# Limiting the expert weight loads in flight to three, in a kernel of chunk attention, a swish layer and a mixture of experts

## The chip, the cores and the metric

The program runs on one core of a Trainium2 chip. The metric is the device time of one execution in microseconds; the time before is the median of three executions.

## What is computed

Three stages, one behind the other, all in float32 (inputs q, k, v of 2 x 8 x 768 x 64):

```python
# 1. attention in chunks of 32 queries: 16 keys to the left, 8 to the right, 8 memory keys
a = softmax(q_c @ concat(mem_k, k_ctx).T / sqrt(D))
x = a @ concat(mem_v, v_ctx)                      # -> 1536 tokens x 512
# 2. a dense layer
h = x @ w_in                                      # 512 x 2048
x = (h * sigmoid(1.702 * h)) @ w_out              # 2048 x 512
# 3. a mixture of 8 experts, top 1, at most 384 tokens for each
e = argmax(x @ w_gate); gate = softmax(x @ w_gate)[e]
y = relu(x_e @ w1[e]) @ w2[e]                     # 512 x 1024, 1024 x 512
out[token] = gate * y
```

## The kernel before, in words

TensorE gets fp32 precision from pairs of a rounded high part and a low part (float32r tiles): each product is three matmuls, high by high, high by low, low by high. So each weight that comes from memory is first turned into such a pair: ScalarE writes the high part (`hi`, L295), VectorE subtracts it from the raw words for the low part (`lo`, L300).

The first two stages take the span up to about 330 us. They run by an order written out by hand (`ORDER`) and by a loop over units of the dense layer. The third stage runs from about 340 us: `expert_parts` makes the pieces of one expert, and the loop at the end of the kernel (L1407) goes through the eight experts. For each it issues the gathers of the next expert's token rows on GpSimd (`load`, L827, an indirect DMA), then the weight loads that have a buffer, and then the expert itself. How many tokens an expert has is known only on the chip, so `both` (L1090) builds the code in two arms under a branch, and at run time every engine branches by itself to one of them: `first_of_two` (L1045), `first_of_narrow` (L1059) or `first_of` (L1037) for the first layer, then `thirds_first` (L1111), `after_arms` (L1142) and `second` (L1148) for the rest. The first layer's results stand in four PSUM buffers (L1389), from which ScalarE and VectorE evict them.

The expert weights are 64 loads (`pieces`, L209) of 512 KB, eight for each expert: four of `w1`, four of `w2`. `w_load` (L228) issues them on SP's queue (L241) into raw buffers taken from `free_raw` (four from L327, four more from L1396). `w_a` (L303) converts the oldest piece in flight and gives its raw buffer back, which is what lets the next load be issued: a load waits at L241 for the VectorE subtraction that last read its buffer. `w_next` (L347) calls this from set places in the arms, so the order of the conversions on ScalarE and VectorE, and of the loads on SP, is fixed when the program is built. `not_before` (L242) is one more wait that already exists, for a gather. From about 340 us on, SP issues nothing but these loads.

`w_state` and `w_back` (L356, L359) let `both` build the second arm from the same state as the first; both arms issue the same loads.

Of the kernel before, what the change touches and what calls it, by code (L numbers as in the profile page):

```python
# [38 lines left out]
AHEAD = 4  # L39
EARLY = 12  # L40
KEEP = 4
KEEPS = (3, 7, 8)
HALF = P // 2
HEAD2 = 2
# [48 lines left out]
def kernel(  # L93
# [40 lines left out]
    def wait_for(i, j):  # L134

        tc.add_manual_dep(i, j.name, mybir.DependencyInfo(mybir.DependencyClass.Sync, mybir.DependencyReason.DATA),
                          reason="wait_for")
# [77 lines left out]
    pool32 = []  # L215
    free_raw = []
    not_before = []

    def w_dst(name, i, z):

        t = where[name][:, z]
        if name[0] == "wi":
            return t.rearrange("p (c f) -> p c f", f=512)[:, :, i * P:(i + 1) * P]
        if name[0] == "wo":
            return t.rearrange("p (c f) -> p c f", f=P)[:, 4 * i:4 * i + 4]
        return t.rearrange("p (c f) -> p c f", f=512)[:, 2 * i:2 * i + 2]

    def w_load():  # L228

        if w_at[0] >= w_end[0]:  # L230
            return False
        name, i, src = pieces[w_at[0]]
        if not w_can_load():
            return False
        if len(name) == 2:
            w_slot(name)
            raw = w_pools["raw"].tile([P, KC, P, 2], I32, tag="raw", name="raw")
            nc.sync.dma_start(out=raw.rearrange("p c f z -> p c (f z)"), in_=src)
        else:
            raw = free_raw.pop(0)  # L240
            dma = nc.sync.dma_start(out=raw, in_=src).ins  # L241
            for i0 in not_before:  # L242
                wait_for(dma, i0)
        w_at[0] += 1
        flight.append(Piece(name=name, i=i, raw=raw))
        return True
# [5 lines left out]
    def w_slot(name):  # L252
        if name not in where and free_slots:
            where[name] = free_slots.pop(0)
        return name in where
# [90 lines left out]

    def w_next(e, keep=KEEP):  # L347

        name, i = (flight[0].name, flight[0].i) if flight else pieces[min(w_at[0], w_end[0] - 1)][:2]
        if not flight or name[1] * 8 + 4 * (name[0] == "w2") + 2 * name[2] + i >= 8 * e + 8 + keep:  # L350
            return False
        w_step()
        w_loads(8 * F // 512)
        return True

    def w_state():  # L356
        return w_at[0], list(flight), list(free_slots), list(free_raw), dict(where), set(ready)

    def w_back(state):  # L359

        w_at[0] = state[0]
        flight[:], free_slots[:], free_raw[:] = state[1:4]
        for now, was in ((where, state[4]), (ready, state[5])):
            now.clear()
            now.update(was)

    def w_loads(n):
        while len(flight) < n and w_load():
            pass

    def w_can_load():
        if w_at[0] >= w_end[0]:
            return False
        name = pieces[w_at[0]][0]
        return bool(name in where or free_slots) if len(name) == 2 else bool(free_raw)
# [440 lines left out]
    def expert_parts(e, ep, tp, cnt):  # L816
# [212 lines left out]
        def steps(part):  # L1029
            while w_next(e, KEEPS[part]):  # L1030
                pass

        def pump_one(i):
            for _ in range(PUMPS1[i]):
                w_next(e, KEEPS[0])

# [8 lines left out]
        def first_of_two():  # L1045
# [3 lines left out]
            for fc in range(F2):  # L1049
# [3 lines left out]
                if fc in PUMPS:  # L1053
                    w_next(e, KEEPS[0])
            with tc.issue_after(after_mm):
# [3 lines left out]
        def first_of_narrow():  # L1059
# [4 lines left out]
            for fc in range(F2):  # L1064
# [17 lines left out]
                if fc in PUMPS:  # L1082
                    w_next(e, KEEPS[0])
            for z in range(2):
# [4 lines left out]

        def both(cond, yes, no):  # L1090

            before = w_state()
            with tc.If(cond) as some:  # L1093
                yes()
            after = w_state()
            w_back(before)
            with some.Else():
                no()
            assert w_state() == after

        def wide_h(b):
# [9 lines left out]
        def thirds_first():  # L1111

            y_of(1 if e == 0 else 0)
            assert NCB == 3
            for b in range(2, NCB):
                hT_of(b)
                xs_of(b)

                def first():
                    both(cnt[ex] > b * P + HALF, lambda: wide_h(b), lambda: small_h(b))  # L1120

                both(cnt[ex] > b * P, first, start2)
            for j in range(F // 512):
                w_free(("w1", e, j))

        def rest(b):

            if b == NCB:
                return
            y_of(b)  # L1130

            def some():
                gate(b)
                both(cnt[ex] > b * P + HALF, lambda: full(b), lambda: small2(b))

            both(cnt[ex] > b * P, some, lambda: skip(b))
# [55 lines left out]
    with ExitStack() as st:  # L1192
# [34 lines left out]
        def after_attention(_):  # L1227
# [24 lines left out]
            a=lambda p: loaded[p].abs(), b=lambda p: loaded[p].max(), f=lambda p: loaded[p].shift(),  # L1252
# [242 lines left out]
```

## Time and profile before

| what | us |
|---|---|
| median of three runs | 531.24 |
| lowest and highest run | 529.93, 532.84 |
| profiled execution, device time | 531.82 |
| its span, first to last instruction | 530.0 |
| TensorE busy (95% of the span) | 505.2 |
| VectorE, ScalarE, GpSimd busy | 317.6, 279.0, 113.6 |

The time of the profiled execution is 1.8 us longer than the span of its instructions. "PE" is TensorE's matmuls and "PEld" its weight loads, "DVE" is VectorE, "ACT" ScalarE, "POOL" GpSimd, "SP" the engine whose queue issues the loads; a "q" behind a name is that engine's sequencer. "issue" as the end of a wait means that the engine waited for nothing the profile shows. The clock column is the granted share of TensorE's full clock: 1.00 is 2.4 GHz, 0.50 is 1.2 GHz.

### The profile page before, as it was taken

To read this page: it belongs to the slowest core of one execution; us is meant where nothing else is said; L and a number is where in the kernel's file an instruction comes from. 1 tells how busy PE (TensorE), PEld (TensorE's weight loads), DVE (VectorE), ACT (ScalarE), POOL (GpSimd) and SP (SyncE) were. 2 spreads that over 40 slices of the span, in tenths; PEclk is the share of its full clock that TensorE was granted. 3 is DMA by queue.
4 is the path that set the end of the run, shared out by engine and by line. 5 is a ranking of instruction groups with operands and counts; after the bars stand their busy time and mean duration, and the time that the engine had idled before them with its cause. 6 is when DMAs were issued, how large, how long until landed. Compare 5 with 4: busy or idle time off the path is not lost. (4 is left out here: it accounts for less than half of the span.)

```text
span 530.0 us, 10749 instructions
## 1 busy us (share of the span) xinstructions
PE 505.2 (95%) x4085; PEld 434.9 (82%) x4089; DVE 317.6 (60%) x633; ACT 279.0 (53%) x573; POOL 113.6 (21%) x108
## 2 busy tenths in 40 slices
PE   8799999999999999999999999999899799969994
PEld 4689898899989998998888888778787688958883
DVE  5999894587982372222256435549345787854851
ACT  2798887856742342212254333557345676645740
POOL 3334442342310120000000000252002322311211
PEclk9899999999999999999999999999999899979998
DMA  8888564043450004000059311499553868973000
GB/s 319 311 305 307 180 217 144 2 160 109 130 160 1 1 1 160 1 0 1 21 163 306 110 40 28 136 329 381 184 182 108 288 239 258 334 251 122 5 28 29
DMA packets 38761, 80.19 MB, mean 151 GB/s; under 512 B 3865, under 2 KB 10009, under 8 KB 38682
## 3 DMA queue, kind: packets, MB, share of 16 engines
q1 hardware_dynamic: 36010, 70.66, 39.0%
q0 software_dynamic: 2672, 8.47, 4.9%
q8 instruction: 50, 0.82, 0.6%
q14 instruction: 29, 0.24, 0.1%
HBM read 69.63 MB, written 9.75 MB: 150 GB/s over the span
## 5 line engine op out<-in xcount | busy, mean ns | idle before, releaser
L547 PEld LDWEIGHTS psh<-xT,w 128*128 128x128 f32 x1152 | 147.0, 188 | 8.3 <-ACT g L566 0.7
L590 PE MATMUL acc<-w,g 128*128 128x512 f32 x576 | 153.0, 400 | 0.0
L547 PE MATMUL psh<-xT,w 128*128 128x256 f32 x1152 | 151.7, 281 | 0.2 <-ACT g L566 0.2
L590 PEld LDWEIGHTS acc<-w,g 128*128 128x128 f32 x576 | 100.7, 188 | 19.4 <-issue 2.1
L562 ACT ACTIVATE sg<-psh 128x256 f32<-128x256 f32 x96 | 36.7, 383 | 126.4 <-PE psh L547 124.4
L300 DVE TENSOR_TENSOR w<-raw,w 128x1024 fp32r<-128x1024 f32 x64 | 76.0, 1221 | 29.7 <-ACT w L295 25.8
L570 DVE TENSOR_TENSOR g<-sg,g 128x256 fp32r<-128x256 f32 x78 | 38.1, 490 | 80.3 <-ACT g L566 77.7
L295 ACT ACTIVATE w<-raw 128x1024 fp32r<-128x1024 f32 x64 | 65.2, 1054 | 5.1 <-PE psy L1002 3.5
L1002 PE MATMUL psy<-w,hT 128*128 128x512 f32 x240 | 60.9, 412 | 5.0 <-issue 5.0
L1002 PEld LDWEIGHTS psy<-w,hT 128*128 128x128 f32 x240 | 46.5, 197 | 16.6 <-issue 5.7
L601 DVE SCALAR_TENSOR_TENSOR x<-acc,x 128x512 f32<-128x512 f32 x36 | 24.1, 685 | 20.8 <-PE acc L590 20.8
L566 ACT ACTIVATE g<-psh 128x256 fp32r<-128x256 f32 x96 | 36.2, 379 | 0.0
L827 POOL DMA_INDIRECT xr<-rows,taker x18 | 24.4, 1358 | 33.9 <-ACTq L1093 18.8
L1072 PE MATMUL psh<-xs,w 128*128 128x256 f32 x96 | 27.8, 290 | 3.7 <-issue 3.7
L1070 PE MATMUL psh<-xs,w 128*128 128x384 f32 x96 | 30.0, 351 | 0.0
L725 POOL DMA_INDIRECT y<-rows,taker x1 | 1.2, 1228 | 123.8 <-DVE cnt_i L732 123.8
L300 POOL TENSOR_TENSOR w<-w,w 128x512 fp32r<-128x512 f32 x12 | 16.8, 1403 | 42.2 <-ACT w L295 42.2
L290 POOL TENSOR_TENSOR w<-w,rest 128x512 int32<-128x512 int32 x13 | 17.6, 1356 | 34.2 <-DVE w L276 28.1
L276 DVE SCALAR_TENSOR_TENSOR w<-raw,w 128x512 int32<-128x512 int32 x32 | 24.7, 778 | 0.3
L265 ACT ACTIVATE w<-raw 128x512 f32<-128x512 f32 x32 | 21.3, 676 | 6.6 <-DMA raw<-in_w_out_dram 5.8
L295 ACT ACTIVATE w<-w 128x512 fp32r<-128x512 f32 x32 | 19.7, 627 | 9.6 <-POOL w L290 5.0
L1012 POOL DMA_INDIRECT out_dram<-y,taker x10 | 12.2, 1224 | 56.0 <-ACT y L1011 32.9
(163 smaller groups left out, 661.2 us busy)
## 6 DMA issues: line engine op xcount, KB each, us to landing
raw<-in_w_dram SPq DMA_DIRECT2D x64, 512.0 KB, 7.0
raw<-in_w_out_dram SPq DMA_DIRECT2D x16, 512.0 KB, 4.6
raw<-in_w_in_dram SPq DMA_DIRECT2D x16, 512.0 KB, 3.7
vt<-in_v_dram SPq DMA_DIRECT2D x12, 512.0 KB, 4.5
kt<-in_k_dram SPq DMA_DIRECT2D x12, 368.0 KB, 5.5
qt<-in_q_dram SPq DMA_DIRECT2D x12, 256.0 KB, 4.6
out_dram<-blank SPq DMA_DIRECT2D x12, 256.0 KB, 2.7
rows<-x SPq DMA_DIRECT2D x5, 520.0 KB, 4.9
```

The source lines that it names most:

```text
L276: nc.vector.scalar_tensor_tensor(out=self.w, in0=self.words()[1], scalar=-0x40000000, in1=self.w, op0=ALU.bitwise_and, op1=ALU.bitwise_or)
L295: nc.scalar.activation(out=w_dst(self.name, self.i, 0), in_=w, func=AF.Copy)
L300: eng.tensor_tensor(out=lo, in0=w, in1=hi.bitcast(F32), op=ALU.subtract)
L547: nc.tensor.matmul(ps, lhsT=w[:, wz, c, i * P:(i + 1) * P], rhs=xT[tb][:, xz, c, :], start=n == 0, stop=n == 3 * KC - 1)
L562: nc.scalar.activation(out=sg_t[u], in_=h_t[u], func=AF.Silu, scale=1.702)
L566: g_last[:1] = [nc.scalar.activation(out=g[:, 0], in_=h_t.pop(u), func=AF.Silu, scale=1.702).ins]
L570: lo = eng.tensor_tensor(out=g[:, 1], in0=sg_t.pop(u), in1=g[:, 0].bitcast(F32), op=ALU.subtract)
L590: nc.tensor.matmul(acc_t[tb][s], lhsT=g[:, gz, s * P:(s + 1) * P], rhs=w[:, wz, wi, :], start=i == 0 and n == 0, stop=u == last_of(k, tb) ...
L827: return nc.gpsimd.indirect_dma_start(out=t, out_offset=None, in_=rows[:, :], in_offset=bass.IndirectOffsetOnAxis(ap=taker[:, b, ex:ex + 1 ...
L1002: nc.tensor.matmul(ps, lhsT=h[:, hz, fc, o:o + P], rhs=w[:, wz, fc % 4, :], start=fc == 0 and n == 0, stop=fc == F2 - 1 and n == 2)
L1070: nc.tensor.matmul(ps[:, :2 * n].rearrange("p (z n) -> p z n", z=2), lhsT=w[:, 0, c, f0:f0 + P], rhs=t[:, :, c, :n], start=c == 0, stop=False)
L1072: mm = nc.tensor.matmul(ps[:, :2 * P], lhsT=w[:, 1, c, f0:f0 + P], rhs=t[:, 0, c, :], start=False, stop=c == KC - 1)
```

## The change

A list `on_way` holds the last expert loads. Each new load waits, besides what it waited for before, until the load three ahead of it in the order has landed; at most three are then in flight. Where two arms of a branch issue a load each, the list keeps both, and what comes behind waits for the one that ran. The order of all instructions stays.

```diff
+ON_WAY = 3
...
     not_before = []
+    on_way = []
...
             raw = free_raw.pop(0)
             dma = nc.sync.dma_start(out=raw, in_=src).ins
-            for i0 in not_before:
+            on_way.append((dma,))
+            for i0 in not_before + [i for some in on_way[:-ON_WAY] for i in some]:
                 wait_for(dma, i0)
+            del on_way[:-ON_WAY]
...
         def both(cond, yes, no):
 
-            before = w_state()
+            before, ways = w_state(), list(on_way)
             with tc.If(cond) as some:
                 yes()
-            after = w_state()
+            after, ways_yes = w_state(), list(on_way)
             w_back(before)
+            on_way[:] = ways
             with some.Else():
                 no()
+            on_way[:] = [a if a == b else a + b for a, b in zip(ways_yes, on_way)]
             assert w_state() == after
```

## Rows read from the trace of the kernel before

**Rows 1.** The page: span and busy time

```profile
span 530.0 us, 10749 instructions
PE 505.2 (95%) x4085; PEld 434.9 (82%) x4089; DVE 317.6 (60%) x633; ACT 279.0 (53%) x573; POOL 113.6 (21%) x108
```

**Rows 2.** Waits of PE, 340 to 530: us in total, times, longest

```profile
PE psy L1002 <- issue: 5.0, 3, 4.4
PE psh L1072 <- issue: 3.7, 1, 3.7
PE psh L918 <- DVE xs L909: 1.5, 1, 1.5
```

**Rows 3.** Timeline of PE at both: start, us, what, [idle before]

```profile
417.63 0.58 PE L1072 MATMUL psh<-xs,w 128*128 128x256 f32 x1 [3.69 <-issue]
...
463.69 1.03 PE L846 MATMUL pst<-ident,xr 128*128 128x128 f32 x8
469.09 1.19 PE L1002 MATMUL psy<-w,hT 128*128 128x512 f32 x2 [4.37 <-issue]
```

**Rows 4.** Windows: PE, PEld, DVE, ACT, POOL busy, PEclk, DMA share, GB/s

```profile
415.30:416.30 1.00, 0.00 (x0) 0.00 (x0) 1.00 (x2) 1.00 (x2) 0.69 (x2) 1.00 0.75 212
416.30:417.60 1.30, 0.00 (x0) 0.00 (x0) 1.30 (x2) 0.79 (x1) 1.30 (x1) 0.86 0.78 145
417.60:420.70 3.10, 3.07 (x12) 3.07 (x13) 2.03 (x3) 0.79 (x2) 0.31 (x1) 0.51 1.00 360
420.70:424.00 3.30, 3.30 (x24) 3.30 (x24) 2.03 (x4) 1.70 (x5) 0.00 (x0) 1.00 1.04 394
...
464.50:466.30 1.80, 0.22 (x3) 0.00 (x0) 1.51 (x3) 1.80 (x4) 0.00 (x0) 1.00 1.05 387
469.10:475.30 6.20, 6.20 (x15) 4.85 (x16) 3.50 (x3) 2.95 (x3) 0.00 (x0) 0.50 0.64 212
475.30:483.10 7.80, 7.80 (x35) 6.14 (x33) 1.45 (x3) 1.82 (x4) 1.01 (x1) 1.00 0.62 197
```

**Rows 5.** DMA queues, 415.3 to 416.3, then 466.3 to 467.5: packets, MB, share

```profile
q8 instruction: 1, 0.02, 6.1%
...
q8 instruction: 1, 0.02, 5.8%
```

**Rows 6.** Loads issued 452 to 460 (seven), then at 406.1, 410.7, 455.3, 459.4

```profile
DMA to landing us min/median/max: 9.2/10.2/10.7
...
DMA to landing us min/median/max: 4.1/4.1/4.1
...
L241 SPq DMA_DIRECT2D raw<-in_w_dram x1: 368/368/368, 410.7 to 410.7; - x1
DMA to landing us min/median/max: 5.1/5.1/5.1
...
L241 SPq DMA_DIRECT2D raw<-in_w_dram x1: 368/368/368, 455.3 to 455.3; - x1
DMA to landing us min/median/max: 10.3/10.3/10.3
...
L241 SPq DMA_DIRECT2D raw<-in_w_dram x1: 367/367/367, 459.4 to 459.4; - x1
```

**Rows 7.** The load issued at 357.4

```profile
DMA to landing us min/median/max: 8.1/8.1/8.1
```

**Rows 8.** Timeline of ACT, 359 to 368

```profile
364.38 2.22 ACT L295 ACTIVATE w<-raw 128x1024 fp32r<-128x1024 f32 x2 [0.27 <-ACTq L1093]
366.81 1.06 ACT L295 ACTIVATE w<-raw 128x1024 fp32r<-128x1024 f32 x1
```

**Rows 9.** PE's lines by form from 363.5 to 374.9: busy us, mean ns

```profile
L879 PE MATMUL psh<-xs,w 128*128 128x256 f32 x96 | 11.7, 283 | 0.0
```

**Rows 10.** Timeline of SP, 196 to 276

```profile
199.73 1.93 SPq L241 DMA_DIRECT2D raw<-in_w_dram  x4
262.10 6.13 SPq L1279 DMA_DIRECT2D out_dram<-blank  x3
```

## The prediction, made before the change was run

> **What bounds the kernel now.** I read the page first: in a span of 530.0 us TensorE is busy for 505.2 [rows 1]. So a change off TensorE's path pays only where TensorE idles, or where its clock is low. The change acts on the expert loads, nearly all of which are issued from 340 us on, so the next view is TensorE's waits from 340 to 530 us. Two waits stand out, 4.37 and 3.69 us, both ended by "issue", which is nothing that the profile names; the next is 1.5 us, for VectorE [rows 2, 3]. No wait of TensorE names a weight conversion or a load's landing. Loads are early enough already; the change can't gain by bringing weights sooner. If it gains, it is in the two "issue" waits.
>
> What are they? In both the engine has just gone into another arm or out of one (at 413.5 it enters `first_of_narrow`, at 464.6 it leaves `first_of_two`), and within each exactly one packet moves on the instruction queue q8: 6.1% and 5.8% of sixteen engines over 1.0 and 1.2 us, that is 0.98 and 1.11 us [rows 5]. I read them as code being fetched. By the Trainium skill (Runtime: NRT & Kernel Launch, "Instruction fetch mechanics") a taken branch whose target is outside the two resident pages must first fetch a page by DMA; the trace agrees, with its one packet in each wait. After each the clock falls to 1.2 GHz: 12 matmuls take 3.07 us at a clock of 0.51, against 24 in 3.30 us at 1.00, a loss of 3.07 - 12 x 0.138 = 1.4 us; 15 take 6.20 us at 0.50, against 35 in 7.80, a loss of 6.20 - 15 x 0.223 = 2.9 us [rows 4]. All that there is to win is 3.7 + 4.4 + 1.4 + 2.9 = 12.4 us.
>
> **The change part by part.** *How many loads it holds.* Taking each load's issue and landing from the trace, 27 of the 64 are issued before the load three ahead has landed. Example: the load at 455.3 lands 10.3 us later, at 465.6; the one three behind it is issued at 459.4 and would now wait until 465.6, 6.2 us more [rows 6]. So the change does what it says, in three bursts (347 to 370, 415 to 423 and 452 to 459 us); elsewhere the wait is met before it is asked.
>
> *What a held load loses.* A load alone lands in 4.1 us, in the burst in 9.2 to 10.7 [rows 6]. The burst's extra is queueing: the DMA moves 387 GB/s there [rows 4], 0.524 MB in 1.35 us. Three in flight, each taking 4.1 us, give one in 1.37 us, practically the same rate. A load that is issued 6 us later would have stood 6 us in the queue, so its landing hardly moves. I cost this at nothing; the cover is the lone load's 4.1 us. If held loads went on taking 8 us, see the second rival.
>
> *What is queued behind the wait.* SP issues nothing but these loads from 340 us on. Early on, the fourth load (issued near 201) would wait some 2.5 us for the first, and behind it SP's next transfer is at 262 [rows 10]: nothing. Some 27 waits on SP's sequencer cost other engines nothing. GpSimd's gathers are on a queue of their own; TensorE waits for none now.
>
> *What the two stalls gain.* At 413.5, TensorE stops; the next held load is the one at 414.8, and the one three ahead of it (issued 410.7) lands 5.1 us later, at 415.8, so it is held 1 us only, and the DMA is not full in this stall (0.75 to 0.78 busy, 145 to 212 GB/s) [rows 4, 6]. Nothing in front of that fetch changes: 0. At 464.6 four loads are in flight and the DMA is full (1.05, 387 GB/s) [rows 4]; with the change three are, and the queue is nearly drained just then. What is a full queue worth to a fetch? The nearest rows are the two stalls themselves: 4.37 us with it full, 3.69 with it three quarters busy [rows 3]. I take the difference, 0.7 us. Upper bound: if the second stall's clock loss shrinks to that of the first, 2.9 - 1.4 = 1.5 us more, 2.2 in all; I do not take it, since a stall of 3.7 us lost clock as well and no row shows a stall of this kind that did not. Lower bound: 0.
>
> Against even the 0.7 speaks the Trainium skill (DMA: Bandwidth & Descriptors, "Queues, rings and completion order"): each DMA engine takes turns between the queues that have work, packet by packet, so the depth of the loads' queue would not hold the fetch back. The trace agrees in part: the packet had moved by 467.5, while the load issued at 459.4, landing after 9.2 us at the earliest, was still under way [rows 5, 6]. By that rule alone the sum would be 0.
>
> The sum: 531.8 (the profiled execution) - 0.7 = 531.1. That execution is 0.6 above the median of 531.24, so for a median I take 530.5.
>
> **The rivals.**
>
> *No effect.* Fetches take turns whatever the depth, and landings stay. For it: the stall at 413.5, nearly as long with the queue not full. Then the time stays at 531.2. It lies within 0.5% as the forecast does, and the two differ only in the second stall.
>
> *A large gain.* The fetch is served only when loads in front of it have moved, and its completion is late for the same reason. Then the second stall is cut to well under half or vanishes with its clock loss: 4.4 + 2.9 = 7.3 us, 524; were the first cut too, 12.4, 519. For it: both stalls lie in a burst. Against it: the first had at most three loads in flight when it began, so three are enough for 3.7 us. Half of the second gone (2.2 + 1.5 = 3.7 us) gives 527.5.
>
> *Slower: three in flight are too few.* In the burst from 347 to 370 us gathers share the DMA, and a load takes 8.1 us [rows 7]. If a held load went on taking that, three would give one in 2.7 us instead of 1.35. The load issued at 357.4 lands at 365.5 and is converted at 366.8 [rows 7, 8], with 1.3 us to spare; from the first held load of this burst to it there are five, so it would be 5 x 1.35 - 1.3 = 5.4 us late. ScalarE works in order, so the evictions behind this conversion (the L882 rows' line) would be late by as much. What covers TensorE are four PSUM buffers of 12 matmuls: 11.7 us for 96 [rows 9], 1.46 each, 5.9 in all if all were free; with half of them free some 2.5 us of stall come through, and the clock loss of one stall (1.4): 535. It decides from the point at which a held load takes over 3 x (1.35 + 1.3 / 5) = 4.8 us. Against it: much of the 8.1 us is queueing behind other loads, which the wait removes.
>
> **How the numbers follow.** Half a per cent (2.7 us) is about what a measurement of this kernel can tell from no change; the three runs before span 2.9 us. Forecast, 0 to 2.2 us gained at the second stall: 0.45. No effect: 0.24, within 0.5% as well. Gain over 2.7 us: 0.21. Slower by over 2.7 us: 0.10. So same 0.69, faster 0.21, slower 0.10. The likeliest case's own range is 529 to 531.5. For 8 in 10 the range has to take in the half form of the gain, 527.5, and the run spread above the median, 532.8; I give 526.5 to 533.
>
> **What would show it right or wrong.** Landings of held loads near 4 to 5 us in the 452 to 459 burst and last landings of the bursts within 1 us of before (the rate holds); the wait at L1002 of 4.4 us down to 3.7 and that at L1072 unchanged at 3.7; no wait of ScalarE at L295 for a landing near 365 us; TensorE's busy time unchanged but for its low clock. Wrong: either stall gone, or a third of its kind at another branch, or landings of held loads still at 8 us with conversions waiting.

## The result and the profile after

The changed kernel is slower: 535.76 us (median of ten executions, 533.18 to 536.84), the kernel before 533.05 beside it on the same chip (ten, 529.52 to 535.41). The ratio is 1.006, 95% interval 1.003 to 1.0089. The forecast was 530.5, and its range, 526.5 to 533.0, does not hold the measured time. All times and ratios below are against the kernel before on the same chip.

The page of the changed kernel, span and busy time (beside [rows 1]). Lines of the changed kernel are two higher than before at the loads (L243) and four higher from the conversions on (L299).

```profile
span 533.8 us, 10746 instructions
PE 507.3 (95%) x4085; PEld 437.0 (82%) x4089; DVE 317.7 (60%) x633; ACT 279.5 (52%) x573; POOL 112.5 (21%) x108
```

The span grew by 3.8 us. TensorE's waits from 340 us on (us in total, times, longest):

```profile
PE psh L883 <- DVE hT L887: 4.7, 1, 4.7
PE psh L1076 <- issue: 3.8, 1, 3.8
PE psy L1006 <- DVE xs L855: 2.5, 1, 2.5
```

Against [rows 2]: the stall at the entry to `first_of_narrow` is where it was (3.7, now 3.8). The one at the way out of `first_of_two`, 4.4 us before, is down to 2.5. But there is a new one of 4.7 us, inside `first_of_two`, in which TensorE waits for `hT`, the evicted result of the first layer. TensorE's timeline at the two places (start, us, what, idle before):

```profile
455.82 2.89 PE L883 MATMUL psh<-xs,w 128*128 128x256 f32 x23
463.43 1.92 PE L883 MATMUL psh<-xs,w 128*128 128x256 f32 x9 [4.71 <-DVE hT L887]
...
474.26 2.04 PE L1006 MATMUL psy<-w,hT 128*128 128x512 f32 x4 [2.48 <-DVE xs L855]
```

Why was `hT` late? ScalarE's timeline in the same stretch:

```profile
453.39 1.05 ACT L299 ACTIVATE w<-raw 128x1024 fp32r<-128x1024 f32 x1
458.59 2.95 ACT L299 ACTIVATE w<-raw 128x1024 fp32r<-128x1024 f32 x3 [4.14 <-DMA raw<-in_w_dram]
461.44 0.36 ACT L886 ACTIVATE hT<-psh 128x256 fp32r<-128x256 f32 x1
461.70 1.04 ACT L299 ACTIVATE w<-raw 128x1024 fp32r<-128x1024 f32 x1
462.65 0.92 ACT L886 ACTIVATE hT<-psh 128x256 fp32r<-128x256 f32 x3
```

It stood 4.14 us in front of a conversion, until 458.59, and came to the first eviction (L886) only behind that conversion and two more, at 461.44. The load it waited for had been issued at 451.2. This is that load's answer (who waited for it, and its time to landing), and behind it that of the three loads issued from 464.2 to 467.3:

```profile
  ACT w L299: 4.1, 1
...
DMA to landing us min/median/max: 7.3/7.3/7.3
...
DMA to landing us min/median/max: 4.3/5.0/5.0
```

The kernel before did not have this conversion in front of the arm. There it is the one at 465.29, behind all evictions of the arm:

```profile
455.22 0.36 ACT L882 ACTIVATE hT<-psh 128x256 fp32r<-128x256 f32 x1
...
464.32 1.08 ACT L850 ACTIVATE xs<-pst 128x512 fp32r<-128x512 f32 x2
465.29 1.06 ACT L295 ACTIVATE w<-raw 128x1024 fp32r<-128x1024 f32 x1
```

So an instruction has changed its place. Comparing the two built programs engine by engine shows how much has moved: nothing on TensorE, VectorE and GpSimd; on SP one load, which comes two places later (near 348 us); and on ScalarE four conversions. This is one of the four (minus: place before; plus: place after):

```
 L1097 UNCONDITIONAL_BRANCH
+L299 ACTIVATE w_1723<-raw_3_3365 128x1024
 L1097 COMPARE_AND_BRANCH
...
 L299 ACTIVATE w_1723<-raw_2_3364 128x1024
 L1097 UNCONDITIONAL_BRANCH
-L299 ACTIVATE w_1723<-raw_3_3365 128x1024
 L860 ACTIVATE ex,gs<-xr 128x8
```

All four are the high part of the fourth piece of the next expert's `w1`, in the third to the sixth expert, and all four went from behind the first layer's arms to ahead of them. The kernel's text fixes the order in which it names its instructions, but the build puts each engine's instructions into an order of its own, and with the added waits that order came out differently (with four loads instead of three, e3, it did not). "The order of all instructions stays", in the section on the change, is wrong.

Where the 3.8 us of the two spans come from, with the clock (columns as in [rows 4]):

```profile
416.20:422.80 6.60, 5.09 (x19) 5.09 (x20) 2.20 (x3) 3.44 (x5) 1.71 (x1) 0.50 1.00 329
...
463.90:467.30 3.40, 3.40 (x19) 3.40 (x18) 2.03 (x4) 0.38 (x1) 0.00 (x0) 0.50 0.96 326
...
474.20:477.50 3.30, 3.24 (x8) 2.59 (x9) 1.81 (x5) 2.44 (x3) 0.00 (x0) 0.50 0.77 214
```

The new wait is +4.7. Behind it the clock is at half (0.50), and the arm's next 48 matmuls take 7.49 us where they took 5.96 before: +1.5 (before, then changed):

```profile
457.89 5.96 PE L879 MATMUL psh<-xs,w 128*128 128x256 f32 x48 [0.29 <-DVE hT L883]
...
463.43 7.49 PE L883 MATMUL psh<-xs,w 128*128 128x256 f32 x48 [4.71 <-DVE hT L887]
```

For the other two places I take the prediction's own prices for a matmul at full clock (0.138 and 0.223 us): the stall at the way out 2.48 - 4.37 = -1.9, and behind it 3.24 - 8 x 0.223 = 1.5 instead of 2.9, -1.4; behind the first stall 5.09 - 19 x 0.138 = 2.5 instead of 1.4, +1.1. The sum is +4.0. The last term is chance as far as the rows show: that stall is as long as before, and in two kernels of the experiments below that change nothing ahead of it, and have it as long (3.5 and 3.6 us), the clock behind it stays at 0.50 until 422.4 us (e8) and 424.4 us (e5).

### The profile page after: what moved, and what is told of

It is laid out like the page before. It is cut to its first block, busy times and chain, and to the rows that moved or that the text cites. A ratio compares the mean times of both kernels' runs of the same rounds, so it can differ in the third digit from the quotient of the medians.

```text
span 533.8 us, 10746 instructions
## 1 busy us (share of the span) xinstructions
PE 507.3 (95%) x4085; PEld 437.0 (82%) x4089; DVE 317.7 (60%) x633; ACT 279.5 (52%) x573; POOL 112.5 (21%) x108
## 5 line engine op out<-in xcount | busy, mean ns | idle before, releaser
L299 ACT ACTIVATE w<-raw 128x1024 fp32r<-128x1024 f32 x64 | 65.4, 1053 | 19.1 <-DMA raw<-in_w_dram 10.3
L1006 PE MATMUL psy<-w,hT 128*128 128x512 f32 x240 | 59.7, 405 | 2.7 <-DVE xs L855 2.5
L1076 PE MATMUL psh<-xs,w 128*128 128x256 f32 x96 | 28.4, 296 | 3.8 <-issue 3.8
L831 POOL DMA_INDIRECT xr<-rows,taker x18 | 22.6, 1254 | 37.4 <-ACTq L1097 21.8
L883 PE MATMUL psh<-xs,w 128*128 128x256 f32 x192 | 25.2, 295 | 4.7 <-DVE hT L887 4.7
L883 PEld LDWEIGHTS psh<-xs,w 128*128 128x128 f32 x192 | 24.5, 201 | 4.9 <-DVE hT L887 4.9
```

What stands on the lines that cost most here:

```text
L299: nc.scalar.activation(out=w_dst(self.name, self.i, 0), in_=w, func=AF.Copy)
L883: mm = nc.tensor.matmul(ps, lhsT=w[:, wz, c, f0:f0 + P], rhs=t[:, xz, c, :], start=m == 0, stop=m == 3 * KC - 1)
L1006: nc.tensor.matmul(ps, lhsT=h[:, hz, fc, o:o + P], rhs=w[:, wz, fc % 4, :], start=fc == 0 and n == 0, stop=fc == F2 - 1 and n == 2)
L1076: mm = nc.tensor.matmul(ps[:, :2 * P], lhsT=w[:, 1, c, f0:f0 + P], rhs=t[:, 0, c, :], start=False, stop=c == KC - 1)
```

## The experiments

Theory A: the four moved conversions are the whole price, and the limit costs nothing. Theory B: the limit itself is the price, by loads that come later. Later, of the stall at the way out of `first_of_two`, theory C (loads in front of the fetch make it long) and theory D (something else does).

### The conversions moved, no limit (e1)

```diff
 def others():
+    if e in HOIST:                       # HOIST = (2, 3, 4, 5)
+        w_slot(flight[0].name)
 ...
+        anchor[:] = [flight[3].hi().name]   # the arms' ScalarE instructions stay behind it
+        flight[3].done = True
     both(cnt[ex] > P + HALF, first_of_two, ...
```

> The kernel before, without any limit on the loads, but ScalarE's conversion of the fourth piece of the next expert's w1 stands ahead of the first layer's arms in the third to sixth experts, as in the changed kernel; every other engine keeps the order of before. Theory A (this reordering is the whole price): TensorE waits 3 to 5 us for hT at L883's counterpart near 458 us, ScalarE idles some 4 us for a load just issued near 415 and 454 us, and the time is 1.003 to 1.009 of before, as the changed kernel's is (1.006). Theory B (the limit on the loads itself is the price): 0.998 to 1.002. The long wait at the entry to first_of_narrow should stay at 3.7 us under both.

Measured: 1.0069 (1.0042 to 1.0095), 536.21 against 532.42 us. TensorE's and ScalarE's waits from 340 us on:

```profile
PE psh L1075 <- issue: 5.5, 1, 5.5
PE psh L882 <- DVE hT L886: 4.5, 1, 4.5
PE psy L1005 <- DVE xs L854: 1.9, 1, 1.9
...
ACT w L297 <- DMA raw<-in_w_dram: 9.1, 2, 5.2
```

Without any limit, the moved conversions alone bring TensorE's wait for `hT` (4.5 us) and ScalarE's waits for loads just issued (5.2 us the longer), and the whole slowdown. Theory A. The 5.5 us at L1075, expected to stay at 3.7, was a miss; the run with three of the conversions (e6) tests whether it comes from them.

### The limit alone, conversions kept behind the arms (e2)

```diff
 def hi(self):
-    nc.scalar.activation(...)
+    hi = nc.scalar.activation(...).ins
+    for name in behind_arm:              # last ScalarE instruction of each arm
+        tc.add_manual_dep(hi, name, ...) # order on the engine only
 ...
+behind_arm[:] = arm_last
```

The order is not quite that of before: in five experts the conversion of this fourth piece comes behind its neighbours, some places later than before, and so does its load on SP. None goes ahead of an arm.

> The changed kernel, three loads under way as there, but the four conversions are kept behind the arms where the kernel before has them; a few neighbours on ScalarE, VectorE and SyncE still change places. Theory A (the reordering is the price, the limit costs nothing): 0.995 to 1.002 of before, no TensorE wait of over 2.5 us for VectorE after 340 us. Theory B (the limit itself): 1.003 to 1.009, with waits of ScalarE for landings of held loads. By the prediction's reading of the stall at the way out of first_of_two, that stall is 3.7 us here instead of 4.4; if the fetch is served only behind the loads, under 2.2 us, and 0.993 of before.

Measured: 0.9996 (0.9974 to 1.0018). The wait for `hT` is gone. The row at the way out of `first_of_two`:

```profile
473.25 2.25 PE L1010 MATMUL psy<-w,hT 128*128 128x512 f32 x7 [3.74 <-DVEq L1101]
```

The limit costs nothing that can be measured: theory B falls. The stall is 3.74 us, what the prediction had taken for three loads under way. The fetch served only behind the loads, in its strong form (under 2.2 us), does not hold at this depth.

### Four ahead instead of three (e3)

```diff
-ON_WAY = 3
+ON_WAY = 4
```

> The changed kernel with one number changed: a load waits for the load four ahead of it instead of three. All engines then have the instruction order of before. Theory A (reordering): 0.996 to 1.002. Theory B (the limit itself, which holds a little less here): 1.001 to 1.005. If the queue in front of a fetch matters, the stall at the way out of first_of_two lies between 4.4 and what three under way give.

Measured: 1.0029 (1.0 to 1.0057), with every engine in the order of before. That is above the 1.002 of theory A, though the interval reaches down to 1.0. SP's waits, 345 to 370 us, and ScalarE and TensorE behind them:

```profile
SPq L243 <- DMA raw<-in_w_dram: 12.8, 2, 12.4
```

```profile
370.59 1.06 ACT L299 ACTIVATE w<-raw 128x1024 fp32r<-128x1024 f32 x1 [3.23 <-DMA raw<-in_w_dram]
```

```profile
374.66 5.57 PE L883 MATMUL psh<-xs,w 128*128 128x256 f32 x32 [2.03 <-DVE hT L887]
...
476.38 2.20 PE L1006 MATMUL psy<-w,hT 128*128 128x512 f32 x7 [3.80 <-DVEq L1097]
```

SP stood 12.4 us at one load (issued at 364.44), until the load issued just ahead of it (351.43) had landed, at 364.36. "Four ahead" counts in the order in which the kernel's text names the loads, and the build issues the fourth piece of `w1` behind its three successors. So here the limit was one load for 12 us, the next conversions came 3.2 us late, and 2.0 us of it came through to TensorE. A price of the limit may thus exist, at the very burst that the prediction's slower rival named, but it comes from the order, not from the depth. The profiled execution (537.86 us) is among the longest of its twelve, so the 2.0 us need not stand in each. The stall at the way out, 3.80 us, lies between 4.37 and e2's 3.74, as expected.

### One moved conversion, and the other three (e4, e6)

```diff
-HOIST = (2, 3, 4, 5)
+HOIST = (5,)            # e4;  (2, 3, 4) in e6
```

> The kernel before, no limit, with one conversion alone ahead of the arms, that of the sixth expert (near 454 us). Theory A in its narrow form (one hoisted conversion, the one followed by TensorE's 4.7 us wait for hT, carries the price): the wait is there and the time is 1.003 to 1.008 of before, as with all four. If each of the four costs its share: about 1.0015. Theory B: 0.998 to 1.002.

> The kernel before, no limit, with the conversion ahead of the arms in the third, fourth and fifth experts alone, the complement of the run with the sixth's. If the prices of the four add: 1.003 to 1.006 of before (1.0069 less 1.0024). If the sixth's, with TensorE's one wait for hT, were all that shows: 0.999 to 1.002. The long stall at the entry to first_of_narrow (near 415 us), which was 5.5 us with all four ahead and 3.7 before, should be over 4.5 us if ScalarE's wait for its load in front of that arm prolongs it, and 3 to 4 if that was a chance.

Measured: 1.0024 (1.0001 to 1.0046) with the sixth expert's alone, 1.0018 (0.9995 to 1.004) with the other three, within the 0.999 to 1.002 expected if those cost nothing. Waits of TensorE (from 340 us on) and of ScalarE (450 to 460 us) in the first, and of TensorE in the second:

```profile
PE psh L882 <- DVE hT L886: 5.0, 2, 4.8
PE psh L1075 <- issue: 3.1, 1, 3.1
PE psy L1005 <- DVE xs L854: 1.8, 1, 1.8
...
ACT w L297 <- DMA raw<-in_w_dram: 4.2, 1, 4.2
```

```profile
PE psy L1005 <- issue: 4.5, 2, 4.3
PE psh L1075 <- issue: 3.8, 1, 3.8
PE psh L965 <- ACT w L297: 1.5, 1, 1.5
```

The sixth expert's conversion alone brings the wait for `hT` (4.8 us), but 1.0024 falls short of the 1.003 to 1.008 expected of it. It also shortens the stall behind it to 1.8 us, because while TensorE stands, the loads run dry (none is under way as the stall begins); so it costs less than its 4.8. The two parts add to 1.0042, the four together measured 1.0069; with these intervals they agree, and the price of the other three cannot be told from nothing. The stall at `first_of_narrow` is 3.8 us with three moved conversions: the 5.5 of e1 does not come from them. In all kernels that hold nothing in front of it, and in those with a limit of two or three, it varied from 3.1 to 5.5 us.

### What the loads do to the stall at the way out of `first_of_two` (e5, e7, e11, e8, e9)

In e5 the last seven loads in question go one at a time (the conversion kept behind the arms):

```diff
+ONE = {("w2", 6, 0), ("w2", 6, 1), ("w1", 7, 0)}
...
-            for i0 in not_before + [i for some in on_way[:-ON_WAY] for i in some]:
+            n = 1 if (name in ONE or (name, i) == (("w1", 7, 1), 0)) else 64
+            for i0 in not_before + [i for some in on_way[:-n] for i in some]:
```

> The kernel before without a general limit; the seven loads from about 452 us on (the last four pieces of the seventh expert's w2 and the first three of the eighth expert's w1) go one at a time, each waiting for the one before, so that one load instead of four is under way when TensorE leaves first_of_two; the conversion that this would move ahead of the arms is kept behind them. All other engines keep the order of before but for one conversion behind its neighbour and one load two places later. If the prediction's reading holds (a fetch is served sooner with a shorter queue in front of it), the stall at the way out of first_of_two falls from 4.4 us (5.0 with the short waits beside it) to at most 3 us, DMA share in it to about a third, and the time is 0.992 to 0.998 of before. If the queue does not matter to a fetch: stall 4 to 5.2 us and 0.998 to 1.002. Held loads land 4 to 5 us after issue; the latest of them is converted 1 us or more after its landing, so no wait of ScalarE for a landing.

Measured: 1.0019 (0.9999 to 1.0039). The stall at the way out, then ScalarE and TensorE 20 us later:

```profile
470.17 2.10 PE L1011 MATMUL psy<-w,hT 128*128 128x512 f32 x8 [2.76 <-ACTq L1102]
...
489.88 0.44 PE L1079 MATMUL psh<-xs,w 128*128 128x384 f32 x1 [1.83 <-DVE low L1085]
```

```profile
488.17 1.06 ACT L301 ACTIVATE w<-raw 128x1024 fp32r<-128x1024 f32 x1 [3.13 <-DMA raw<-in_w_dram]
```

The stall fell as expected of a shorter queue, from 4.4 to 2.76 us. The time is a miss against 0.992 to 0.998, and so is the expected 1 us to spare at the last conversion: seven loads one behind the other came too late for it by 3.1 us, and 1.8 of this came through to TensorE.

Two under way from the start (conversions kept behind the arms; a few gate instructions of one expert come earlier as well), run twice:

```diff
-ON_WAY = 3
+ON_WAY = 2
```

> Two loads under way instead of three, conversions kept behind the arms. Theory A (the limit costs nothing as long as loads land before their conversions): a load alone lands in 4.1 us, so two give one in 2.05 us; 16 loads of an expert take 33 us against some 37 us between experts, but within the burst from 347 us on five loads take 10.3 us instead of 6.8, so ScalarE waits 3 to 6 us near 366 us, and TensorE comes to wait for hT by 0 to 3 us there: 0.999 to 1.008 of before. If each load under way less costs a fixed share (theory B, the limit itself): no more than 1.002 after the 0.9996 with three. The stall at the way out of first_of_two: 4 to 5.2 us if the queue does not matter to a fetch, under 3.7 if it does.

> Two loads under way from the start, conversions kept behind the arms, a second time with more rounds (0.9972 [0.9942, 1.0003] the first time). Theory C with its price at the first burst: 0.995 to 0.999. If the first result was chance: 0.999 to 1.003.

Measured: 0.9972 (0.9942 to 1.0003) and 0.9954 (0.9927 to 0.9981). The stall in the first of them:

```profile
470.55 2.79 PE L1010 MATMUL psy<-w,hT 128*128 128x512 f32 x11 [2.29 <-ACTq L1101]
```

In the second it is 1.73 us. Neither theory A's 3 to 6 us of waiting on ScalarE (1.8 at the longest, at 372 us) nor theory B fits; the stall answers to the queue. (An expert has eight loads, not the sixteen of the expectation.)

Then three loads alone held (one more two at a time), the order of every engine unchanged:

```diff
+LIMITS = {(("w2", 6, 0), 1): 1,
+            (("w2", 6, 1), 0): 1,
+            (("w2", 6, 1), 1): 1,
+            (("w1", 7, 0), 0): 2}
...
+            n = LIMITS.get((name, i), 64)
+            for i0 in not_before + [i for some in on_way[:-n] for i in some]:
```

> The kernel before with nothing held but three loads near the end, the second, third and fourth piece of the seventh expert's w2, which go one at a time (and one more, two at a time); every engine keeps its order exactly. So far the stall at the way out of first_of_two went with the loads under way when it began: four 4.4, 4.35 and 3.8 us, three 3.7, two 2.3, none 2.8. Theory C (a fetch waits for the loads that stand in front of it): one load under way here, stall 2 to 3 us, time 0.995 to 0.999 of before. Theory D (the stall's length follows from what else moved in those kernels, not from the queue): 4 to 4.5 us and 0.999 to 1.002. No wait of ScalarE for a landing of a held load.

Measured: 0.9945 (0.992 to 0.9971), faster than both kernels, and a little faster than theory C's 0.995 to 0.999. TensorE at the place, the DMA share ahead of the stall and the clock behind it, and the code fetch (DMA queues from 465.2 to 466.4 us):

```profile
467.98 3.27 PE L1010 MATMUL psy<-w,hT 128*128 128x512 f32 x13 [1.56 <-DVE xs L859]
```

```profile
464.50:466.40 1.90, 1.90 (x17) 1.68 (x16) 0.82 (x2) 0.81 (x3) 0.00 (x0) 1.00 0.14 50
...
468.00:472.00 4.00, 4.00 (x17) 3.26 (x18) 3.62 (x5) 3.20 (x6) 1.67 (x1) 1.00 0.57 157
```

```profile
q8 instruction: 1, 0.02, 5.5%
```

Just before the stall the DMA is busy by 0.14 (1.05 before, [rows 4]). The packet of the fetch has moved before TensorE comes to its stall at 466.42; in the kernel before it moved some 1.6 us into it [rows 5]. The stall is 1.56 us instead of 4.37, what it still waits for has a name (VectorE), and the clock behind it is 1.00 where it was 0.50. Theory C; with the order unchanged, theory D has nothing left to point to.

By the rows this is 2.8 us of stall and 2.8 us of clock. The ratio gives 1.5 to 4.3 us. Of the difference, 0.9 us is a new wait that ends at 481.94 us (L1078, ended by "issue"); the rest is not explained.

Two under way only from 407 us on (the table `LIMITS` with 26 loads at 2, conversions kept behind the arms):

> Two loads under way at most, but only in the last 26 loads that matter (from about 407 us on); before that no limit, and the conversions are kept behind the arms. Against two from the start it leaves out the burst from 347 to 370 us, where ScalarE waited 0.1 to 1.8 us for loads. Theory C: stall at the way out of first_of_two 2 to 3 us, time 0.994 to 0.999 of before. Theory D: 0.999 to 1.002.

Measured: 0.9991 (0.9965 to 1.0017), a miss against 0.994 to 0.999, though the stall fell to 2.72 us. Its profiled execution has 5.1 us at `first_of_narrow`. Why it gains less than two from the start is open.

The stall by the loads under way as it begins (from issue and landing of each load; for e9 and e11 the limit), with the start of the fetch's packet, counted from the moment TensorE stops (minus: ahead of it); one trace for each kernel, e10 and e12 from below:

| loads | kernels | stall, us | packet's start, us |
|---|---|---|---|
| four | before, e6, e3 | 4.37, 4.35, 3.80 | 1.61, 1.60, 0.93 |
| three | e2 | 3.74 | 1.12 |
| two | e9, e7, e11 | 2.72, 2.29, 1.73 | -0.19, -0.34, -0.97 |
| one, or one just being issued | e5, the changed kernel, e10, e8, e12 | 2.76, 2.48, 1.66, 1.56, 1.45 | 0.19, -0.20, -1.16, -1.14, -1.15 |
| none (TensorE stood before) | e1, e4 | 1.88, 1.84 | -1.15, -1.15 |

In all fourteen traces TensorE goes on 2.6 to 3.0 us after this packet starts, whatever the profile names as the end of the wait. So the loads set when the packet starts, and this sets the stall; 1.5 to 1.9 us of it are left when nothing or little stands in front. The tie to the packet rests on this steady distance. A packet within a wait, from which the prediction read the fetch, is no sign by itself: in the kernel before, 25 of them move on q8 from 340 to 530 us, and two of them come with a long "issue" wait.

### Both stalls (e10, e12)

To e8's table come two loads near 412 us, `(("w1", 4, 1), 0): 1` and `(("w1", 4, 1), 1): 1`, and the conversion that this would move is kept behind its arm.

> As the run with three held loads, and besides the third and fourth piece of the fifth expert's w1 (issued near 411 and 412 us before) go one at a time, so that one load instead of two is under way when TensorE enters first_of_narrow near 414 us; the conversion that this would move is kept behind its arm. Theory C for both stalls: the one at first_of_narrow falls from 3.7 to 2.5 to 3.2 us, the other to 2 to 3 us, and the time is 0.992 to 0.998 of before. If the first stall is not made by loads: 3.1 to 5.5 us as in all runs so far, and the time as with the three held loads alone.

> The kernel with five loads held around both stalls a second time, since its first eight executions spread over 10 us. If one load less in front of the fetch at first_of_narrow is worth about 1 us (2.7 us against 3.1 to 5.5 in all other kernels) on top of the three held loads (0.9945): 0.990 to 0.994 of before. If the 2.7 us were chance: 0.992 to 0.997, with that stall between 3.1 and 5.5 us.

Measured: 0.9914 (0.9879 to 0.9948) and, the same kernel again, 0.9948 (0.9918 to 0.9978); the executions of the first spread over 10 us (the median of all eight, 530.28 us, is 0.994 of 533.24), so I go by the second. The stall at `first_of_narrow` in the first run, then in the second, where the other one follows:

```profile
418.56 0.58 PE L1086 MATMUL psh<-xs,w 128*128 128x256 f32 x1 [2.74 <-issue]
```

```profile
418.35 0.39 PE L1086 MATMUL psh<-xs,w 128*128 128x256 f32 x1 [0.45 <-issue]
...
467.70 2.56 PE L1016 MATMUL psy<-w,hT 128*128 128x512 f32 x10 [1.45 <-DVE xs L865]
```

2.74 and 0.45 us are the two shortest of all kernels, 3.1 to 5.5 elsewhere. But they do not show that this stall too answers to the weight loads. In the second run the fetch's packet starts at 416.08 us, about as in the first (416.15) and in e8 (416.47); it is TensorE that comes late. It had waited 1.9 us for VectorE and done the 18 matmuls behind that in 5.99 us instead of e8's 4.42:

```profile
402.42 5.99 PE L976 MATMUL psh<-w,xs 128*128 128x512 f32 x18 [1.89 <-DVE y L958]
```

So it stops at 417.90 instead of 415.30 and goes on at 418.35, in e8 at 418.82: the short wait is mostly time lost earlier. And with at most two weight loads under way this stall is 4.0 (e7) and 5.1 us (e9); gathers are on the DMA there too (34.9% beside the loads' 33.6% from 415.3 to 416.3 us in the kernel before). TensorE goes on 2.2 to 2.5 us after the packet's start here, in all fourteen traces; what makes the packet late at this place is open. In the time nothing shows: 0.9948 is no better than the 0.9945 with three loads held.

## Why the prediction was wrong

*The step that failed* is the paragraph "What is queued behind the wait", which puts it at nothing: "Some 27 waits on SP's sequencer cost other engines nothing." It took from the description of the change that the order of all instructions stays, and counted only what stands behind SP's wait at run time. But the waits also went into the order that the build gives to the other engines, and ScalarE came to stand up to 4.2 us in front of loads just issued, with the evictions behind it. A move of four conversions, without any limit, costs 0.69% (e1); the limit, without the moves, -0.04% (e2). The changed kernel's +0.6% is the one with the other.

*What bounds the kernel* was read rightly: a gain lies only in the two "issue" waits and the clock behind them. e8 took 2.8 us of stall and the half clock behind it away, and gained 0.55%, about half of what the rows price them at.

*The gain of 0.7 us at the second stall* came out as priced, 3.74 us at three loads (e2) against 4.37, but with some luck: it was the difference between two stalls at different places, at the first of which TensorE goes on 2.3 us after the packet starts and at the second 2.8, and with four loads under way e3 shows 3.80. In the changed kernel the same place shows 2.48, but that is because TensorE's new wait had let the queue drain. The bound of 2.2 us in all was too narrow for a queue of one: e8's stall alone is 2.8 us shorter. *The first stall, 0*, holds: 3.77 against 3.69, in both with two loads under way and a third issued 0.3 us before it.

*The doubt about the 0.7*: the fetch's packet started 0.9 to 1.6 us into the stall with four loads under way, 1.1 with three (e2), 0.2 to 1.0 ahead of it with two, and 0.2 into it (e5) to 1.2 ahead with one. The Trainium skill (DMA: Bandwidth & Descriptors, "Queues, rings and completion order") has each DMA engine take turns between the queues that have work. By that rule alone the sum would have been 0, and these packets' starts do not agree with that. Which part of the path makes the packet wait is not shown.

*What a held load loses.* The forecast of 4 to 5 us to landing in the burst near the end holds for its last three loads (4.3 to 5.0 us, issued from 464.2 us on), not for the three issued from 457.2 to 461.2, which took 5.9 to 7.3. That is still longer than the 4.1 us of a load alone [rows 6]. The forecast that the last landing of each burst stays within 1 us failed in the burst from 347 us on: its last load landed at 384.7 us instead of 377.5; near the end it is 472.2 instead of 469.5, behind TensorE's new wait. The late landing in the first burst cost TensorE nothing; ScalarE stood 2.0 us before a conversion:

```profile
368.82 1.06 ACT L299 ACTIVATE w<-raw 128x1024 fp32r<-128x1024 f32 x1 [2.02 <-DMA raw<-in_w_dram]
```

*The rivals.* "No effect" is what the limit alone does (e2). "A large gain" was right about the mechanism and wrong about the dose: it is there at one or two loads under way and not at three. "Slower: three in flight are too few" has the sign of the result, and its place was seen (2.0 us of ScalarE near 366 us instead of the 5.4 it took), but it is not the cause: its stall was to come near 366 us and came at 459. That the build reorders other engines was not among the rivals; the prediction's "So the change does what it says" was the place to ask for it, and I did not.

## What to carry to other kernels

A wait added to one queue is an input to whatever orders the other engines: compare the built instruction lists of all engines before costing it at nothing, and keep moved instructions in place by an order on their own engine. An engine on which work on a fresh load gets an early place pays the load's whole time to landing, here 7.3 us, less what stood in front of it, and the work behind it pays too. Where a branch must fetch code, hold back the few bulk loads that would stand in front of the fetch: three held loads gave 0.55%, a limit of two everywhere 0.28 and 0.46%, a limit of three everywhere nothing.

## What was not expected of the hardware

At the way out of `first_of_two`, the stall at a code fetch goes with the depth of the weight loads' queue: 3.8 to 4.4 us with four loads of 512 KB under way, 3.7 with three, 1.7 to 2.7 with two, 1.5 to 2.8 with one. In the one trace with three the price of the fetch is nearly that with four; only two or one brought it down. At the entry to `first_of_narrow` the same was not seen. How the loads hold the packet back was not tried.
